# Strassen blocks in interleaved pairs, with half-bank sums, two sets of product banks and combinations on GpSimd

## The chip, the core and the metric

The kernel runs on one core of one Trainium2 chip. A core has TensorE (PE; its weight loads are shown as PEld), VectorE (DVE), ScalarE (ACT), GpSimd (POOL) and SyncE (SP, which issues DMAs). They run on their own, each takes its instructions in order, and semaphores join them. TensorE writes to PSUM alone: eight banks of 128 partitions by 512 fp32 values. ACT and DVE read PSUM, POOL doesn't. The metric is the device time of one execution in microseconds (us).

## What is computed

```python
X = np.fft.rfft(x, axis=1)                      # x: (4, 3008, 256)
Yr = Xr @ w_r - Xi @ w_i + b_r
Yi = Xr @ w_i + Xi @ w_r + b_i
Y  = shrink(Yr, 0.01) + 1j * shrink(Yi, 0.01)   # sign(v) * max(|v| - 0.01, 0)
y  = np.fft.irfft(Y, n=3008, axis=1)
h  = y.reshape(12032, 256) @ w_in               # 256 -> 2048
g  = h * sigmoid(h)                             # Silu
out = g @ w_out                                 # 2048 -> 256
```

## The kernel before

A spectral stage (DFTs as matmuls, a complex mix, the inverse DFT) feeds an MLP. The MLP takes the 12032 tokens in 24 blocks of 512 (the last, `LAST` = 23, has 256). Products are made from fp32 values split in a high and a low part (`gh`, `gl`; `win[0]`, `win[1]`), and three of the four part products are summed.

The main loop at the end of the kernel counts **ticks**: one tick is one block `i` and one `f`, a slice of 128 of the 2048 hidden features, so a block has 16 ticks. In a tick of a plain block `mlp1` makes `h` (six matmuls of 512 columns), ACT takes Silu, and in the next tick `split_g` makes `gh` (ACT) and `gl` (DVE). Then `mlp2` adds this slice to the output sums: for each 128 tokens (below: a **unit**) a 512-column matmul of `gh` with the high and the low part of `w_out` side by side (L665), and a 256-column one of `gl` (L669). So the sum of 128 tokens fills one PSUM bank, a block needs all four `acc` banks, and at the end of the block ACT copies one half and DVE adds the other (L685, L686). The banks: four `acc`, two `h`, two `d` for all else.

Spectral work for later blocks is placed in ticks by `at` and `put`: `i2` and `i2_ends` make the MLP's input of the next block (matmuls at L470; ACT and DVE split the result, and for late blocks ACT also copies it to `xf`).

The six blocks 17 to 22 (`FAST`) make `h` by Strassen's scheme: seven products of half size in place of eight. A **pair** is two `f` (q = 0 to 7), and its products live in two banks, `px` and `py`. `fast_one` (even tick) makes four products, 12 matmuls of 256 columns; then ACT copies `u` (L615) and DVE makes three sums (L616 to L618). `fast_two` (odd tick) adds three more products into the same banks, 9 matmuls, so it must wait until ACT and DVE have read them; then come a Silu (L627), two sums (L628, L629), a Silu (L630), a cast (L636), the low part (L634, called `low`), and the same for the other half (L638, L639). Both `h` banks are in use all the time. The moving combinations (`fast_moving`, once in a block: four sums on DVE, a cast on ACT, one low part on DVE) and the weight combinations (`fast_weights`, eight times before the first such block, one in each tick) are fillers too. In these blocks the sums of a tick's `f` run two ticks later, four units in every tick.

Of the kernel before, what the change touches and what calls it, by code (L numbers as in the profile page):

```python
# [116 lines left out]
def spectral_mlp_kernel(ctx: ExitStack, tc: tile.TileContext, x, w_r, w_i, b_r, b_i, w_in, w_out, c1, c2, c3, c4, c3f, c5, out):  # L117
# [24 lines left out]
    def bank(name):  # L142

        tag, bufs = "d", 2
        if state["prologue"]:
            state["d"] = (state["d"] + 1) % 4
            tag, bufs = (("d", 2), ("acc", 4), ("h", 2), ("acc", 4))[state["d"]]
        return ps.tile([128, 512], F32, tag=tag, bufs=bufs, name=name)
# [371 lines left out]
    LAST = len(BLOCKS) - 1  # L520

# [23 lines left out]
    def split_g(i, f):  # L545
# [7 lines left out]
        gf[i, f] = (gh, gl)  # L553

    HB = BLK // 2
    xf, th, tw, fast = {}, {}, {}, {}

    def fast_weights(q):

        k = slice(q * 256, (q + 1) * 256)  # L560
        f32 = tl.tile([128, 2, 256], F32, tag="td", bufs=1, name="wf")
        d = tl.tile([128, 4, 128], F32, tag="wd", bufs=2, name="wd")
# [15 lines left out]
    def fast_moving(i):  # L578
# [3 lines left out]
        l0, r0, l1, r1 = x32[:, 0, 0:HB], x32[:, 0, HB:BLK], x32[:, 1, 0:HB], x32[:, 1, HB:BLK]  # L582
        nc.vector.tensor_sub(d[:, 0, :], r0, l0)
        nc.vector.tensor_sub(d[:, 2, :], r1, r0)
        nc.vector.tensor_sub(d[:, 1, :], r1, d[:, 0, :])
        nc.vector.tensor_sub(d[:, 3, :], l1, d[:, 1, :])
        yield
        hi = tl.tile([128, 4, HB], F32R, tag="th", bufs=2, name="th")
        lo = tl.tile([128, 4, HB], F32R, tag="tl", bufs=2, name="tl")
        nc.scalar.copy(hi, d)  # L590
        yield
        nc.vector.tensor_sub(lo, d, hi)
        th[i] = (hi, lo)
# [12 lines left out]
    def fast_one(i, q):  # L606

        px, py = [ps.tile([128, 512], F32, tag="h", bufs=2, name="h") for _ in range(2)]
# [5 lines left out]
        g = tl.tile([128, 4, HB], F32, tag="gp", bufs=2, name="gp")  # L614
# [4 lines left out]
        fast[i, q] = (px, py, u, g)  # L619

    def fast_two(i, q):

        px, py, u, g = fast.pop((i, q))
# [7 lines left out]
        gs = [tuple(tl.tile([128, 2, HB], F32R, tag=f"g{k}", bufs=4, name=f"g{k}") for k in "hl") for _ in range(2)]  # L631

        def low(r):
            nc.vector.tensor_sub(gs[r][1], g[:, 2 * r:2 * r + 2, :], gs[r][0])  # L634

        nc.scalar.copy(gs[0][0], g[:, 0:2, :])  # L636
        low(0)
        nc.scalar.activation(out=g[:, 2:4, :], in_=g[:, 2:4, :], func=ACTF.Silu)  # L638
        nc.scalar.copy(gs[1][0], g[:, 2:4, :])  # L639
        later.append(lambda: low(1))  # L640
        for r in range(2):
            gf[i, 2 * q + r] = tuple(v.rearrange("p a c -> p (a c)") for v in gs[r])

    later = []
# [3 lines left out]
    def mlp2(i, f):  # L648
        n = BLOCKS[i][1]
        gh, gl = gf.pop((i, f))  # L650
        begins = f == 0 or (i, f) == (0, 8)
        ends = f == NFF - 1 or (i, f) == (0, 7)
        for t in range(n // 128):
            if begins:
                acc[i, t] = ps.tile([128, 512], F32, tag="acc", bufs=4, name="acc")
            a = acc[i, t]
            q = slice(t * 128, (t + 1) * 128)
            if i == LAST:
                for m, (v, k) in enumerate(((gh, 0), (gh, 1), (gl, 0))):
                    nc.tensor.matmul(  # L660
                        out=a[:, 0:D], lhsT=v[:, q], rhs=wout[:, f, k, :],
                        start=(f == 0 and m == 0), stop=(f == NFF - 1 and m == 2),
                    )
                continue
# [8 lines left out]
        if ends:  # L673
            for t in range(n // 128):
                a = acc.pop((i, t))
                half = x_sb[1][:, t * D:(t + 1) * D]
                if f == 7:
                    nc.scalar.copy(half, a[:, D:2 * D])
                    nc.vector.tensor_tensor(out=half, in0=a[:, 0:D], in1=half, op=ALU.add)
                    continue  # L680
                o = sb.tile([128, D], F32, tag="o", bufs=5, name="o")
                if i == LAST:
                    (nc.vector.tensor_copy if t % 2 else nc.scalar.copy)(out=o, in_=a[:, 0:D])
                else:
                    nc.scalar.copy(o, a[:, D:2 * D])  # L685
                    nc.vector.tensor_tensor(out=o, in0=a[:, 0:D], in1=o, op=ALU.add)  # L686
                if i == 0:
                    nc.vector.tensor_add(o, o, half)
                for k, b, j, p0, m in pieces(BLOCKS[i][0] + t * 128, 128):
                    v = out[b * S:(b + 1) * S].rearrange("(p j) d -> j p d", j=NJ)  # L690
                    store(v[j, p0:p0 + m, :], o[k:k + m, :])
# [50 lines left out]
    with tc.manual_schedule():  # L742
# [169 lines left out]
        for i in range(1, len(BLOCKS)):  # L912
# [6 lines left out]
            if i in FAST:  # L919
                moving = fast_moving(i)  # L920
                for k in range(3):
                    at(t + 2 + k, next, moving, None)
# [38 lines left out]
        done = 0  # L961
        for t in range(len(ticks) + 2):
            i, f = ticks[t] if t < len(ticks) else (LAST, None)
            if 0 <= t - 1 < len(ticks) and ticks[t - 1][0] not in FAST:
# [3 lines left out]
            if i in FAST:  # L968
                (fast_two if f % 2 else fast_one)(i, f // 2)
            elif t < len(ticks):  # L970
                mlp1(i, f)
            if f is None or i not in FAST or f % 2 == 0:
                while later:
                    later.pop(0)()
            for fn, args in fill.pop(t, []):
                fn(*args)
            flush(1 if t < 12 else 4)
# [33 lines left out]
```

## Time and profile before

| | |
|---|---|
| time, median of 3 runs | 1383.92 us (1381.0 to 1384.56) |
| the profiled execution | 1383.38 us; span 1381.3 us, 21395 instructions |
| PE busy | 1350.9 us, 98% of the span, granted clock 0.997 |
| DVE busy | 809.9 us, 59% |
| ACT busy | 767.9 us, 56% |
| POOL busy | 125.9 us, 9% |

The times are of one profiled execution, measured from the span's start. A matmul's duration in the trace includes the time in which its results drain, in which the next one already runs; so the distance between two starts is the pace, and the busy share of PE counts short pauses as work. A bracket at the end of a row of the timeline gives the idle time of the engine ahead of it and what ended it.

### The profile page before, as it was taken

What the parts mean: (1) busy time and instruction counts of PE and PEld (TensorE: products, weight loads), DVE (VectorE), ACT (ScalarE), POOL (GpSimd) and SP (SyncE); (2) the same over time, 40 slices, a digit from 0 to 9 for tenths busy, and PEclk for the clock granted to TensorE, in tenths of its full rate; (3) what the DMA queues carried; (4) which work ended last, traced back from release to release, by engine and by line L of the source; (5) the groups of instructions that cost most, each with busy time, mean ns of one, the idle gap of its engine ahead of it and who ended that gap; (6) DMA issues with size and microseconds to landing.
All of it is one profiled execution on the core that took longest, in us unless ns stands there. A gap on an engine that the chain in (4) does not pass through costs nothing.

```text
span 1381.3 us, 21395 instructions
## 1 busy us (share of the span) xinstructions
PE 1350.9 (98%) x8021; PEld 1175.2 (85%) x8021; DVE 809.9 (59%) x1518; ACT 767.9 (56%) x1552; POOL 125.9 (9%) x192
## 2 busy tenths in 40 slices
PE   8999999999999999999999999999999999999998
PEld 3977888888888888888888888888888888888898
DVE  3767756565665365666644455555464666666663
ACT  5446555455777455657555445554455555555554
POOL 2001002221111012221100011111000000000000
PEclk9999999999999999999999999999999999999999
DMA  8876324231543232524233212121210100010001
GB/s 266 256 228 185 111 58 117 59 89 37 128 119 99 84 88 72 143 64 104 68 88 79 67 49 80 54 77 30 59 27 7 32 28 25 3 39 16 1 16 24
DMA packets 72759, 109.81 MB, mean 79 GB/s; under 512 B 8400, under 2 KB 54224, under 8 KB 72656
## 3 DMA queue, kind: packets, MB, share of 16 engines
q1 hardware_dynamic: 58537, 79.07, 20.1%
q0 software_dynamic: 10544, 25.68, 7.2%
q10 hardware_dynamic: 3575, 3.70, 0.9%
q8 instruction: 63, 1.03, 0.3%
q14 instruction: 40, 0.33, 0.1%
HBM read 70.93 MB, written 37.49 MB: 78 GB/s over the span
## 4 chain that ended last, share of the span: by engine, by line
PE 82%; ACT 7%; DVE 6%; DMA 3%; issue 2%; DVEq 0%; SPq 0%; ACTq 0%
PE h L535 28%; PE acc L665 21%; PE acc L669 10%; PE mix L380 6%; PE h L602 5%; PE i L470 3%; PE s L355 2%; PE i L428 2%; PE mix L319 2%; ACT gh L636 1%; PE s L258 1%; DVE gp L617 1%; DVE u L616 1%; ACT gp L630 1%; DVE gp L628 1%
## 5 line engine op out<-in xcount | busy, mean ns | idle before, releaser
L665 PE MATMUL acc<-wout,gh 128*128 128x512 f32 x1472 | 540.1, 401 | 1.1 <-DVE o L686 1.1
L535 PE MATMUL h<-xt,win 128*128 128x512 f32 (+1 forms) x1728 | 436.4, 388 | 0.0
L669 PE MATMUL acc<-wout,gl 128*128 128x256 f32 x1472 | 412.4, 280 | 0.2 <-DVE gl L552 0.2
L542 ACT ACTIVATE g<-h 128x512 f32<-128x512 f32 (+1 forms) x289 | 168.7, 584 | 362.3 <-PE h L535 360.4
L535 PEld LDWEIGHTS h<-xt,win 128*128 128x128 f32 x1728 | 299.8, 188 | 61.0 <-DVE xt L487 0.4
L665 PEld LDWEIGHTS acc<-wout,gh 128*128 128x128 f32 x1472 | 277.2, 188 | 57.3 <-DVE o L686 1.7
L552 DVE TENSOR_TENSOR gl<-g,gh 128x512 fp32r<-128x512 f32 (+1 forms) x289 | 198.1, 688 | 183.5 <-ACT gh L551 180.7
L669 PEld LDWEIGHTS acc<-wout,gl 128*128 128x128 f32 x1472 | 278.0, 189 | 6.9 <-DVE gl L552 0.6
L551 ACT CAST gh<-g 128x512 fp32r<-128x512 f32 (+1 forms) x289 | 175.7, 608 | 2.8
L634 DVE TENSOR_TENSOR gl<-gp,gh 128x512 fp32r<-128x512 f32 x96 | 65.9, 687 | 39.3 <-ACT gh L636 38.8
L387 POOL TENSOR_TENSOR q<-q,bias 128x256 f32<-128x256 f32 x36 | 26.4, 734 | 570.0 <-ACT q L386 570.0
L602 PE MATMUL h<-xt,win 128*128 128x256 f32 x288 | 53.5, 294 | 16.7 <-DVE gp L617 16.6
L260 DVE TENSOR_TENSOR s1o<-s,s1o 48x512 f32<-48x512 f32 x64 | 41.0, 678 | 48.3 <-ACT s1o L259 47.3
L602 PEld LDWEIGHTS h<-xt,win 128*128 128x128 f32 x288 | 40.4, 188 | 30.2 <-issue 26.9
L627 ACT ACTIVATE gp<-h 128x256 f32<-128x256 f32 x48 | 18.4, 384 | 84.7 <-PE h L602 84.7
L487 DVE TENSOR_TENSOR xt<-i,xt 128x376 fp32r<-128x376 f32 (+2 forms) x48 | 28.1, 586 | 61.5 <-ACT xt L486 57.6
L400 DVE TENSOR_TENSOR y<-q,mix 64x256 f32<-64x256 f32 x144 | 60.3, 419 | 2.1
L470 PEld LDWEIGHTS i<-c_sb,gin 96*128 96x128 f32 x420 | 54.0, 193 | 8.0 <-issue 4.1
L365 DVE TENSOR_TENSOR xs<-s,xs 128x256 f32<-128x256 f32 x36 | 15.3, 424 | 71.9 <-ACT xs L364 71.9
L470 PE MATMUL i<-c_sb,gin 96*128 96x94 f32 x420 | 53.9, 273 | 3.1 <-DMA gin<-scr 3.1
L249 DVE TENSOR_TENSOR sx<-x_sb,sx 47x1024 fp32r<-47x1024 f32 x32 | 40.7, 1271 | 22.3 <-ACT sx L248 22.3
L188 POOL DMA_DIRECT2D x_sb<-in_x_dram x64 | 32.7, 513 | 142.6 <-ACT sx L248 125.5
(168 smaller groups left out, 1991.1 us busy)
## 6 DMA issues: line engine op xcount, KB each, us to landing
a<-scr SPq DMA_DIRECT2D x48, 256.0 KB
x_sb<-in_x_dram POOLq DMA_DIRECT2D x64, 188.0 KB, 3.5
gin<-scr SPq DMA_DIRECT2D x30, 384.0 KB
t<-in_c_dram POOLq DMA_DIRECT2D x36, 256.0 KB, 3.1
scr<-i1o SPq DMA_DIRECT2D x36, 256.0 KB
t<-in_c_dram SPq DMA_DIRECT2D x48, 128.0 KB
scr<-s1o SPq DMA_DIRECT2D x32, 192.0 KB
scr<-s1o SPq DMA_DIRECT2D x13, 384.0 KB
```

The lines of the kernel that those rows point to most:

```text
L260: nc.vector.tensor_tensor(out=o[:, c], in0=p[:2 * NR, :], in1=o[:, c], op=ALU.add)
L380: nc.tensor.matmul(out=out, lhsT=x_[:, e, c, :], rhs=m[:, e, :], start=(n == 0), stop=(n == 5))
L400: nc.vector.tensor_tensor(out=y[64 * i:64 * i + 64, r, :], in0=q[rows, i, :], in1=pv[rows, i, :], op=op,)
L470: nc.tensor.matmul(out=p[:, o:o + m], lhsT=g_t[b, j // 4][:, q:q + 128], rhs=c4_sb[:, p0:p0 + m], start=True, stop=True,)
L535: nc.tensor.matmul(out=p[:, :n], lhsT=w[:, e, f * 128:(f + 1) * 128], rhs=v[:, e, :n], start=(m == 0), stop=(m == 5),)
L542: nc.scalar.activation(out=g[:, q], in_=p[:, q], func=ACTF.Silu)
L551: nc.scalar.copy(gh[:, q], g[:, q])
L552: nc.vector.tensor_sub(gl[:, q], g[:, q], gh[:, q])
L602: nc.tensor.matmul(out=p, lhsT=w[j], rhs=m[k], start=(begins and n == 0), stop=(n == 2), skip_group_check=True,)
L634: nc.vector.tensor_sub(gs[r][1], g[:, 2 * r:2 * r + 2, :], gs[r][0])
L665: nc.tensor.matmul(out=a, lhsT=gh[:, q], rhs=wout[:, f].rearrange("p a c -> p (a c)"), start=begins, stop=False,)
L669: nc.tensor.matmul(out=a[:, D:2 * D], lhsT=gl[:, q], rhs=wout[:, f, 0, :], start=False, stop=ends,)
```

## The change

Blocks 15 to 23 (`NARROW`) keep the sums of two units in one bank: three matmuls of 256 columns write the same half bank, and the bank is emptied after its second unit by two ACT copies, with no DVE add. These blocks use two `acc` banks (`acc0`). The other two (`acc1`) are a second set for `px` and `py`: even pairs use `h`, odd pairs `acc1`. In the main loop a pair's `fast_two` is issued after the next pair's `fast_one`, with two units between; units are a list and are issued by twos. The second half of a pair's Silu, cast and low part (`parts(1)`) comes one tick later. The moving combinations go to GpSimd as eight instructions of 256 columns in eight ticks, with two ACT casts. The weight combinations are spread over more ticks (eight pairs in 11 ticks in place of 7) and use the ring of `gp` buffers, which has three in place of two.

```diff
+    NARROW = [FAST[0] - 2, FAST[0] - 1, *FAST, LAST]
...
+        def low(k):
+            nc.gpsimd.tensor_sub(lo[:, k, :], d[:, k, :], hi[:, k, :])
+
+        nc.gpsimd.tensor_sub(d[:, 0, :], r0, l0)
+        yield
+        nc.gpsimd.tensor_sub(d[:, 1, :], r1, d[:, 0, :])
+        yield
+        nc.gpsimd.tensor_sub(d[:, 2, :], r1, r0)
+        nc.scalar.copy(hi[:, 0:2, :], d[:, 0:2, :])
+        yield
+        low(0)
...
     def fast_one(i, q):
 
-        px, py = [ps.tile([128, 512], F32, tag="h", bufs=2, name="h") for _ in range(2)]
+        tag = ("h", "acc1")[q % 2]
+        px, py = [ps.tile([128, 512], F32, tag=tag, bufs=2, name="h") for _ in range(2)]
...
-    def fast_two(i, q):
-
-        px, py, u, g = fast.pop((i, q))
+        fast.append((i, q, px, py, u, g))
+
+    def fast_two():
+
+        i, q, px, py, u, g = fast.pop(0)
...
+        narrow = i in NARROW
+        k = t // 2 if narrow else t
+        if begins and not (narrow and t % 2):
+            tag = "acc0" if narrow or t % 2 == 0 else "acc1"
+            acc[i, k] = ps.tile([128, 512], F32, tag=tag, bufs=2, name="acc")
...
+        if narrow:
+            a = a[:, t % 2 * D:(t % 2 + 1) * D]
+            for m, (v, w) in enumerate(((gh, 0), (gh, 1), (gl, 0))):
+                nc.tensor.matmul(
+                    out=a, lhsT=v[:, q], rhs=wout[:, f, w, :],
+                    start=(f == 0 and m == 0 and t % 2 == 0), stop=(ends and m == 2), skip_group_check=True,
+                )
...
+        if ends and narrow and t % 2:
+            a = acc.pop((i, k))
+            for v in range(2):
                 o = sb.tile([128, D], F32, tag="o", bufs=5, name="o")
...
+                (nc.vector.tensor_copy if i == LAST and v else nc.scalar.copy)(out=o, in_=a[:, v * D:(v + 1) * D])
+                output(i, t - 1 + v, o)
...
-                at(last + 2 + q + k, next, steps, None)
-        assert last + 11 < 16 * FAST[0]
+                at(last + 2 + q * 8 // 5 + k, next, steps, None)
...
             if i in FAST:
-                (fast_two if f % 2 else fast_one)(i, f // 2)
...
+                if f % 2 == 0:
+                    fast_one(i, f // 2)
+                    if t == first_fast:
+                        run(2)
+                    else:
+                        if t > first_fast + 2:
+                            run(2)
+                        fast_two()
+                        run(2)
+                else:
+                    run(2)
+                    while later:
+                        later.pop(0)()
+                    if t > first_fast + 3:
+                        run(2)
+                fills(t)
+                continue
```

Up to the first unit of block 15 the order of every engine is the one before. Three places show what moved. The first is PE inside block 17, from the last matmul of a `fast_one` (`tl`, `sw_h`) to the first of a `fast_two` (`xt`, `win`). Before:

```order
L602 MATMUL h<-tl,sw_h_10341 128x256
L665 MATMUL acc<-wout,gh 128x512
L669 MATMUL acc<-wout,gl 128x256
L665 MATMUL acc<-wout,gh 128x512
L669 MATMUL acc<-wout,gl 128x256
L665 MATMUL acc<-wout,gh 128x512
L669 MATMUL acc<-wout,gl 128x256
L665 MATMUL acc<-wout,gh 128x512
L669 MATMUL acc<-wout,gl 128x256
L602 MATMUL h<-xt_10451,win_83 128x256 [waits DVE_49,Activation_49]
```

After:

```order
L617 MATMUL h<-tl,sw_h_10610 128x256
L682 MATMUL acc<-wout,gh 128x256 [waits Activation_49]
L682 MATMUL acc<-wout,gh 128x256
L682 MATMUL acc<-wout,gl 128x256 [waits DVE_49]
L682 MATMUL acc<-wout,gh 128x256 x2
L682 MATMUL acc<-wout,gl 128x256
L617 MATMUL h<-xt_10486,win_83 128x256
```

Two units stand there now where four stood, and the `fast_two` behind them is that of the pair before; its first matmul carries no wait.

The second place is DVE in one pair of block 17 (`u`, `gp`, `h` with their numbers, so that pairs can be told apart). Before, the sums of a `fast_one`, an old `low`, the sums of the same pair's `fast_two` and its first `low`:

```order
L616 TENSOR_TENSOR u_10988<-h_10975,u_10988 128x256 [waits PE_49,Activation_49]
L617 TENSOR_TENSOR gp_10989<-h_10974,u_10988 128x256 [waits DVE_49]
L618 TENSOR_TENSOR gp_10989<-h_10975,gp_10989 128x256 [waits DVE_49]
L634 TENSOR_TENSOR gl_10952<-gp_10918,gh_10951 128x512
L628 TENSOR_TENSOR gp_10989<-h_10974,u_10988 128x256 [waits Activation_49]
L629 TENSOR_TENSOR gp_10989<-h_10975,u_10988 128x256 [waits PE_49]
L634 TENSOR_TENSOR gl_11017<-gp_10989,gh_11016 128x512 [waits Activation_49]
```

After:

```order
L632 TENSOR_TENSOR u_11085<-h_11072,u_11085 128x256 [waits PE_49,Activation_49]
L633 TENSOR_TENSOR gp_11086<-h_11071,u_11085 128x256 [waits DVE_49]
L634 TENSOR_TENSOR gp_11086<-h_11072,gp_11086 128x256 [waits DVE_49]
L644 TENSOR_TENSOR gp_11009<-h_10994,u_11008 128x256 [waits Activation_49]
L645 TENSOR_TENSOR gp_11009<-h_10995,u_11008 128x256 [waits PE_49]
L654 TENSOR_TENSOR gl_11111<-gp_11009,gh_11110 128x512 [waits Activation_49]
L654 TENSOR_TENSOR gl_11127<-gp_11009,gh_11126 128x512 [waits DVE_49,Activation_49]
```

The two sums at L644 and L645 now belong to the pair before (11009) and stand behind the three sums of the new pair (11086).

The third place is DVE at the end of block 15, where its sums (`acc`) are emptied while weight combinations (`wf`, `wd`, `sw_l`) are made. Before:

```order
L575 TENSOR_TENSOR sw_l_10342<-wd,sw_h_10341 128x512 [waits DMAHW7_49,DMAHW0_49]
L563 TENSOR_TENSOR wf<-win_83,win_84 128x512 [waits DVE_49]
L566 TENSOR_TENSOR wd<-wf 128x128 [waits DVE_49]
L567 TENSOR_TENSOR wd<-wd,wf 128x128 [waits DVE_49]
L568 TENSOR_TENSOR wd<-wf 128x128
L569 TENSOR_TENSOR wd<-wf,wd 128x128 [waits DVE_49]
L686 TENSOR_TENSOR o<-acc,o 128x256 [waits DMAHW5_49,DMAHW6_49,DMAHW4_49,Activation_49]
```

After:

```order
L571 TENSOR_TENSOR wd<-wf,wd 128x128 [waits DVE_49]
L553 TENSOR_TENSOR gl<-g,gh 128x512 [waits PE_49,Activation_49] x2
L577 TENSOR_TENSOR sw_l_10412<-wd,sw_h_10411 128x512 [waits DMAHW7_49,DMAHW0_49,DVE_49]
L565 TENSOR_TENSOR wf<-win_83,win_84 128x2x256
L568 TENSOR_TENSOR wd<-wf 128x128 [waits DVE_49]
```

The adds of the output sums are gone from DVE, and one or two low parts (`gl`) stand between two weight combinations.

## Rows read from the trace of the kernel before

**Rows 1.** Busy time by stretch, blocks 17 to 22: start:end, us, engines, PEclk, DMA.

```profile
1056.70:1348.50 291.80, 275.11 (x1879) 248.58 (x1878) 186.70 (x405) 162.53 (x362) 0.00 (x0) 1.00 0.07 20
```

**Rows 2.** Waits, 1000 to 1381.3 us: engine line, waited for, us in total, times, longest.

```profile
PE h L602 <- DVE gp L617: 16.6, 27, 1.2
```

**Rows 3.** Timeline of PE: start, us, engine, line, operation, count, idle before.

```profile
1117.89 0.51 PE L602 MATMUL h<-xt,win 128*128 128x256 f32 x3
...
1119.32 0.40 PE L665 MATMUL acc<-wout,gh 128*128 128x512 f32 x1
...
1122.12 0.59 PE L602 MATMUL h<-xt,win 128*128 128x256 f32 x3 [1.23 <-DVE gp L617]
...
1123.26 1.03 PE L470 MATMUL i<-c_sb,gin 96*128 96x94 f32 x8
1124.07 0.47 PE L665 MATMUL acc<-wout,gh 128*128 128x512 f32 x1
...
1125.54 0.52 PE L602 MATMUL h<-xt,win 128*128 128x256 f32 x3
...
1340.17 0.40 PE L665 MATMUL acc<-wout,gh 128*128 128x512 f32 x1
...
1341.58 0.53 PE L602 MATMUL h<-xt,win 128*128 128x256 f32 x3
```

**Rows 4.** Instructions by line, 1056.7 to 1348.5 us; then line L470 there.

```profile
L665 PE MATMUL acc<-wout,gh 128*128 128x512 f32 x378 | 139.1, 402 | 0.0
...
1056.70:1348.50 291.80, 15.23 (x116) 14.43 (x116) 1.00 0.07 20
```

**Rows 5.** Timeline of ACT and of DVE around that wait.

```profile
1119.22 0.47 ACT L486 CAST xt<-i 128x376 fp32r<-128x376 f32 x1
...
1120.68 0.38 ACT L615 COPY u<-h 128x256 f32<-128x256 f32 x1
...
1123.97 0.42 ACT L630 ACTIVATE gp<-gp 128x256 f32<-128x256 f32 x1 [0.49 <-DVE gp L628]
1124.42 0.62 ACT L636 CAST gh<-gp 128x512 fp32r<-128x512 f32 x1
1124.95 0.63 ACT L638 ACTIVATE gp<-gp 128x512 f32<-128x512 f32 x1
1125.61 0.62 ACT L639 CAST gh<-gp 128x512 fp32r<-128x512 f32 x1
...
1121.09 0.42 DVE L616 TENSOR_TENSOR u<-h,u 128x256 f32<-128x256 f32 x1 [0.81 <-ACT u L615]
1121.55 0.42 DVE L617 TENSOR_TENSOR gp<-h,u 128x256 f32<-128x256 f32 x1
1122.01 0.42 DVE L618 TENSOR_TENSOR gp<-h,gp 128x256 f32<-128x256 f32 x1
1122.35 0.68 DVE L634 TENSOR_TENSOR gl<-gp,gh 128x512 fp32r<-128x512 f32 x1
1123.52 0.42 DVE L628 TENSOR_TENSOR gp<-h,u 128x256 f32<-128x256 f32 x1 [0.49 <-ACT gp L627]
...
1125.08 0.69 DVE L634 TENSOR_TENSOR gl<-gp,gh 128x512 fp32r<-128x512 f32 x1 [0.81 <-ACT gh L636]
```

**Rows 6.** Timeline of PE, end of block 15.

```profile
1013.69 1.55 PE L535 MATMUL h<-xt,win 128*128 128x512 f32 x6
1016.35 0.50 PE L665 MATMUL acc<-wout,gh 128*128 128x512 f32 x1 [1.12 <-DVE o L686]
```

**Rows 7.** One line each: duration in ns min/median/max, first and last start, forms.

```profile
L388 POOL TENSOR_TENSOR q<-q,bias x36: 741/1068/1075, 198.9 to 966.9; 128x256 f32<-128x256 f32 x36
...
L249 DVE TENSOR_TENSOR sx<-x_sb,sx x32: 1222/1222/1744, 299.3 to 741.6; 47x1024 fp32r<-47x1024 f32 x32
```

**Rows 8.** Chain that ended last, 1370 us to the end: start, us, what.

```profile
1373.56 0.72 PE acc L660 x6
...
1377.19 0.42 DVE o L683
```

More of the change, by code (lines that the diff above doesn't have):

```diff
@@ L630, in fast_two @@
         nc.scalar.activation(out=g[:, 1, :], in_=g[:, 1, :], func=ACTF.Silu)
[L631 to L640, printed above, removed]
@@ L641, in fast_two, with parts @@
-        for r in range(2):
-            gf[i, 2 * q + r] = tuple(v.rearrange("p a c -> p (a c)") for v in gs[r])
+        def parts(r):
+            h, l = [tl.tile([128, 2, HB], F32R, tag=f"g{k}", bufs=4, name=f"g{k}") for k in "hl"]
+            v = g[:, 2 * r:2 * r + 2, :]
+            if r:
+                nc.scalar.activation(out=v, in_=v, func=ACTF.Silu)
+            nc.scalar.copy(h, v)
+            nc.vector.tensor_sub(l, v, h)
+            gf[i, 2 * q + r] = tuple(a.rearrange("p a c -> p (a c)") for a in (h, l))
+            units.extend((i, 2 * q + r, t) for t in range(BLK // 128))
@@ L644, in spectral_mlp_kernel, with mlp2 @@
+        parts(0)
+        later.append(lambda: parts(1))
+    units = []
     later = []
     acc = {}
-    def mlp2(i, f):
+    def mlp2(i, f, t):
         n = BLOCKS[i][1]
-        gh, gl = gf.pop((i, f))
+        gh, gl = gf[i, f]
+        last = t == n // 128 - 1
         begins = f == 0 or (i, f) == (0, 8)
         ends = f == NFF - 1 or (i, f) == (0, 7)
[L653 to L664, printed above, removed]
+        narrow = i in NARROW
[3 more added lines that the diff above has]
+            acc[i, k] = ps.tile([128, 512], F32, tag=tag, bufs=2, name="acc")
+        a = acc[i, k]
+        q = slice(t * 128, (t + 1) * 128)
+        if narrow:
[6 more added lines that the diff above has]
+        else:
@@ L920, in spectral_mlp_kernel @@
                 moving = fast_moving(i)
[L921 to L922 removed]
+                for k in range(8):
+                    at(t + 1 + k, next, moving, None)
+                assert t + 8 < 16 * i
         for t, n in enumerate(W_GO):
@@ L957, in spectral_mlp_kernel, with fills, run @@
             for k in range(3):
-                at(last + 2 + q + k, next, steps, None)
-        assert last + 11 < 16 * FAST[0]
-        done = 0
-        for t in range(len(ticks) + 2):
+                at(last + 2 + q * 8 // 5 + k, next, steps, None)
+        assert last + 2 + 11 + 2 < 16 * FAST[0]
+        def fills(t):
+            for fn, args in fill.pop(t, []):
+                fn(*args)
+            flush(1 if t < 12 else 4)
+        def run(n):
+            for v in units[:n]:
+                mlp2(*v)
+            del units[:n]
+        first_fast, last_fast = 16 * FAST[0], 16 * (FAST[-1] + 1)
+        for t in range(len(ticks) + 1):
             i, f = ticks[t] if t < len(ticks) else (LAST, None)
-            if 0 <= t - 1 < len(ticks) and ticks[t - 1][0] not in FAST:
+            if t and ticks[t - 1][0] not in FAST:
                 split_g(*ticks[t - 1])
```

81 lines of the change are left out of this document (42 added, 39 removed).

## The prediction

> **What bounds the kernel now.** I read the busy time by stretch first, then the waits, then the timeline of PE where it waits, then ACT and DVE there. The clock is at its full 2.4 GHz level in blocks 17 to 22 (granted 1.00 [rows 1]), so pauses, not the clock, are what can be saved there. In this stretch of 291.8 us PE is busy 275.1, DVE 186.7 and ACT 162.5 [rows 1]: no engine but PE is near its limit. The view of waits puts 16.6 us on DVE's sum L617, 27 times [rows 2]: `fast_two` waits until the sums have read the banks that it adds to.
>
> A busy PE hides part of this, since a matmul's bar outlasts the start of the next. So I count work at pace, from starts. The 12 matmuls of a `fast_one` take 1119.32 - 1117.89 = 1.43 us, so a `fast_two` with 9 takes 1.07 and a pair 2.50 [rows 3]; 6 blocks of 8 pairs make 120.0. Four units take 1341.58 - 1340.17 = 1.41 us [rows 3], 0.3525 each; 378 of them [rows 4] make 133.2. The 116 matmuls at L470 [rows 4] go by eight in 0.81 us (1123.26 to 1124.07), and the four units behind them take 1.47 (to 1125.54), 0.06 more [rows 3]; with 17 such places (three per next block, two for the last) that is 11.7 + 1.0 = 12.7. Work at pace: 265.9. **PE waits 291.8 - 265.9 = 25.9 us here**, more than the view of waits says. Starts are rounded to 0.01 us, which leaves about 1.7 either way on this count.
>
> Why it waits: from the last unit at pace (1119.32 + 1.41 = 1120.73) to the `fast_two` at 1122.12 are 1.4 us [rows 3]. ACT copied `u` at 1120.68, late because it had to do the next block's input first (1119.22), and DVE's three sums follow at 1121.09, 1121.55, 1122.01 [rows 5]. Between `fast_one` and its own `fast_two` only four units cover that.
>
> **The change, part by part.**
>
> *Interleaving, second bank set.* A `fast_two` now comes after the next `fast_one`, which needs other banks. Between the sums' data and their use lie a whole pair's work, 5.4 us: the wait goes, if ACT and DVE keep up on average. What is late next? I work out two things, the cover and the ring.
>
> Cover. From the end of a `fast_two` at pace (1123.26) to the end of its first `low` (1125.08 + 0.69 = 1125.77) are 2.51 us [rows 5]. Now six units (2.16 at 0.36) and a `fast_one` (1.43) come before the first unit that reads it, and that unit's third matmul is 0.24 later: 3.83. Spare: 1.3 us. The banks are free earlier: the last sum that reads them, L629, is behind L628 (1123.52), so done about 1.0 us after the end, and the `fast_one` that takes them starts 2.16 after it. Spare: 1.1.
>
> Ring. ACT and DVE now hold each other in a ring over pairs: `u` (ACT), three sums (DVE), L628's sum of the pair before, Silu, cast, Silu, cast (ACT), next `u`. By starts in rows 5: 0.41 + 0.46 + 0.46 + 0.34 (to the next DVE operation) + 0.45 + 0.45 + 0.53 + 0.66 + 0.53 = 4.29 us. PE needs 2.50 + 8 x 0.36 = 5.38 for a pair. So in a plain pair the ring is 1.1 faster. Next-block input adds 1.46 to the ring (1119.22 to 1120.68 [rows 5]) and 0.9 to PE: 5.75 against 6.28, good. Where the output copies of a block fall in too (once per block, tick 3; four copies at the 0.38 of the `u` copy, which has their shape, 1.52), it is 7.27 against 6.28: the ring falls back 1.0, just inside the spare of 1.1 to 1.3, and the next pairs win it back. So nearly all of the 25.9 goes. I leave 2.0 us for places where the spare runs out and for the start and the end of the stretch; bounds 0 and, as a rival, 11.
>
> *Half-bank sums.* A unit is three matmuls of 256 in place of 512 + 256, the same columns and one more weight load. The last block does it already: six such matmuls, two units, in 0.72 us [rows 8], 0.36 a unit against 0.3525. Eight blocks of 64 units, 512 x 0.0075 = **3.8 us more**; at the pace of `fast_one` (1.43/12 = 0.119 a matmul) it would be 0.3575 a unit and 2.6 us, the lower bound. The weight loads stay hidden in that row. The TensorE page of the Trainium skill ("TensorE: Matmul & The Clock Gate", Back-to-back issue gap) gives N/2.4 + 2.5 ns: by it a unit would go from 325 to 327.5 ns, my estimate 1.3 us in all, and the time 1359.9; the rows show 352 and 360, and they decide.
>
> *Emptying the banks.* Four DVE adds less per block; ACT keeps four copies. At the end of block 15 PE now waits for such an add: six matmuls of 512 from 1013.69 take 1.39 at the pace of 0.23, and the next starts at 1016.35, **1.3 us late** [rows 6]. DVE was behind with the weight combinations, one in every tick. Now the add is gone and the combinations are spread: this goes, and the spreading costs nothing, since it ends before block 17 and DVE has room. With two units in a bank the first copy waits 0.36 us for the second unit; the next block's first unit is a `fast_one` and two units away, so that is hidden. At the very end it isn't: both copies read one bank now and stand one behind the other, while DVE's copy (0.42 from 1377.19 [rows 8]) had a bank of its own. **0.4 us more**, up to 0.5.
>
> *Combinations on GpSimd.* DVE loses four sums and a long low part, 2.9 us per block; ACT's cast becomes two of about 0.53 pitch. GpSimd gets eight instructions per block. The like one there takes 741 to 1075 ns [rows 7], so 5.9 to 8.6 us, over eight ticks of 2.7 (21.6). They are done before the block that needs them starts, and no other work waits on that queue by then. They may hold DVE up, below.
>
> **Sum**, against the profiled execution (1383.4; the median is 0.5 above): 1383.4 - 25.9 - 1.3 + 3.8 + 0.4 + 2.0 = 1362.4. I say **1362**.
>
> **The rivals.**
>
> *The ring binds beside the fillers.* GpSimd and DVE get in each other's way: where a GpSimd instruction ran, DVE's L249 rose from 1222 to 1744 ns, and L388 on GpSimd from 741 to 1068 [rows 7]. So a DVE operation with two inputs in SBUF (the `low`s) can be 0.5 us late. The four pairs of a block that carry the next input, the copies or combinations would lose their spare and then wait about one such hold-up: 5 blocks x 4 pairs x 0.55 = 11 us in place of 2: **1371**. For it: my ring is 1.0 over in one pair already. Against: the combinations come from tick 8 on, after that pair, where the ring is 1.1 ahead. The Trainium skill ("SBUF — State Buffer", Who interferes with whom) calls this an exclusive lock, held for a whole instruction, between GpSimd and a DVE instruction with two SBUF inputs. By that rule the later one blocks fully; the 0.52 in the row is most of one 0.74 us instruction, so the trace agrees.
>
> *The waits only move.* If PE's order still meets ACT and DVE in step (say, a `fast_one` waiting for banks as long as `fast_two` did), what goes is the 1.3, and the 3.8 and 0.4 stay: 1383.4 - 1.3 + 4.2, about **1386**, within the noise. Against: the spare of 1.1 us above.
>
> *Slower.* One mechanism: the ring becomes the pace of every pair. At my ring with fillers (4.29 + (2 x 1.46 + 1.52 + 1.84 for the block's ends, an input's half and a copy + 2 x 0.53)/8 = 5.2) it isn't; PE's mean with fillers is (120.0 + 384 x 0.36 + 12.7)/48 = 5.6. Above 5.6 each 0.1 costs 48 x 0.1 = 4.8 us. To be 0.3% slower (1387.5) takes 25.5 us, a ring of 6.2, that is 1.0 in every pair on top of the rows: two hold-ups of the size of L249's in each pair, where GpSimd has one instruction per pair on average. Time at that point: **1388**.
>
> **How the numbers follow.** Forecast, nearly all waits gone, 1358 to 1366: 0.64. Ring binds beside fillers, 1366 to 1377: 0.22. Waits move, 1379 to 1387: 0.08. Slower: 0.05. Faster than 1358: 0.01. The range takes in the bounds (1357.5: without the 2.0, with 2.6 for the units, and with 1.7 more of waits) and reaches into the second case: 1357.5 to 1372. About 0.3% is what a measurement of this kernel can tell from no change (1379.8 to 1388.1): faster 0.87, same 0.08, slower 0.05.
>
> **What would show it.** In the profile after: the stretch of blocks 17 to 22 lasts about 270 us; `fast_two` follows the units with no idle time named after DVE; four units take 1.44 us; the pause at the end of block 15 is gone; GpSimd's combinations take 0.7 to 1.1 us and no matmul waits for them. Wrong it would be if matmuls of `fast_one` or units show idle time that ends with ACT or DVE in most pairs, or if the units take more than 0.37.

## The result and the profile after

The changed kernel takes **1360.51 us** in the median of 4 runs (1358.07 to 1364.06), beside 1383.51 for the kernel before: a ratio of 0.9838, 95% interval 0.9812 to 0.9865. The profiled execution took 1361.32 us, its span is 1359.5; against the profiled execution of before that is 22.1 us less. The forecast was 1362.0 in a range of 1357.5 to 1372.0.

Two lines of the page of the kernel after: busy time by engine, and the shares of the chain that ended last.

```profile
PE 1346.2 (99%) x8533; PEld 1203.7 (89%) x8533; DVE 787.0 (58%) x1456; ACT 766.8 (56%) x1558; POOL 163.9 (12%) x240
...
PE 96%; DMA 2%; ACT 1%; DVE 0%; issue 0%; SPq 0%; ACTq 0%
```

PE has 512 matmuls more and is busy 4.7 us less: a bar lasts 0.28 us where the next start comes after 0.12, and ahead of a pause, of which there are fewer now, the rest counts as busy. The chain hardly leaves PE. The view of waits of the kernel after has no row for PE at all from 1000 us to the end, where before it had 16.6 us in 27 waits of `fast_two` [rows 2]. The stretch of blocks 17 to 22, busy time as in [rows 1]:

```profile
1056.60:1327.50 270.90, 270.90 (x2267) 270.80 (x2267) 168.72 (x356) 162.16 (x368) 31.01 (x40) 1.00 0.08 22
```

270.9 us in place of 291.8, PE busy from end to end, and the clock at 1.00 in both. The timeline of PE in block 18 of the kernel after, behind the `fast_two` of the pair that waits in [rows 3]: six units, four filler matmuls, a `fast_one`, two units, the `fast_two` of the pair before.

```profile
1119.48 0.40 PE L682 MATMUL acc<-wout,gh 128*128 128x256 f32 x2
...
1121.64 0.58 PE L470 MATMUL i2e<-c_sb,gin 96*128 96x94 f32 x4
1122.01 0.60 PE L617 MATMUL h<-xt,win 128*128 128x256 f32 x3
...
1123.52 0.40 PE L682 MATMUL acc<-wout,gh 128*128 128x256 f32 x2
...
1124.24 0.52 PE L617 MATMUL h<-xt,win 128*128 128x256 f32 x3
...
1125.32 0.40 PE L682 MATMUL acc<-wout,gh 128*128 128x256 f32 x2
```

No row has a bracket: nothing is waited for. Six units take 1121.64 - 1119.48 = 2.16, which is 0.36 each; the `fast_two` takes 1.08. ACT and DVE at the same place (compare [rows 5]):

```profile
1118.27 0.38 ACT L631 COPY u<-h 128x256 f32<-128x256 f32 x1
1119.32 0.38 ACT L643 ACTIVATE gp<-h 128x256 f32<-128x256 f32 x1 [0.68 <-PE h L617]
...
1124.08 0.39 ACT L631 COPY u<-h 128x256 f32<-128x256 f32 x1
...
1121.49 0.69 DVE L654 TENSOR_TENSOR gl<-gp,gh 128x512 fp32r<-128x512 f32 x1 [0.80 <-ACT gh L653]
```

The low part of the `fast_two` that ended at 1119.48 is done at 1121.49 + 0.69 = 1122.18, and the first matmul that reads it is the third of the unit at 1123.52, at 1123.76: 1.6 us to spare. ACT is the one that waits, 0.68 us for PE. At the end of block 15 (compare [rows 6]) the pause is gone, six matmuls of 512 columns and then the next unit 1.39 later:

```profile
1014.50 1.55 PE L536 MATMUL h<-xt,win 128*128 128x512 f32 x6
1015.89 0.40 PE L682 MATMUL acc<-wout,gh 128*128 128x256 f32 x2
```

The end of the chain that ended last (compare [rows 8]), where two copies of one bank now stand one behind the other:

```profile
1352.79 2.17 PE acc L682 x18
1354.96 0.02 issue
1354.98 0.38 ACT o L701
1355.37 0.02 issue
1355.39 0.42 DVE o L701
```

And one line each of a combination on GpSimd and of the `low`s on DVE (duration in ns min/median/max, as in [rows 7]):

```profile
L594 POOL TENSOR_TENSOR td<-xf,td x6: 735/739/1062, 1034.9 to 1261.9; 128x256 f32<-128x256 f32 x6
...
L654 DVE TENSOR_TENSOR gl<-gp,gh x96: 691/692/850, 1064.1 to 1330.4; 128x512 fp32r<-128x512 f32 x96
```

So the forecast held. Whether it held for its own reasons is what the experiments ask.

### The profile page after: what moved, and what is told of

The parts are those of the page before. It is cut to its first block, busy times and chain, and to the rows that moved or that the text cites. A ratio compares the mean times of both kernels' runs of the same rounds, so it can differ in the third digit from the quotient of the medians.

```text
span 1359.5 us, 22374 instructions
## 1 busy us (share of the span) xinstructions
PE 1346.2 (99%) x8533; PEld 1203.7 (89%) x8533; DVE 787.0 (58%) x1456; ACT 766.8 (56%) x1558; POOL 163.9 (12%) x240
## 4 chain that ended last, share of the span: by engine, by line
PE 96%; DMA 2%; ACT 1%; DVE 0%; issue 0%; SPq 0%; ACTq 0%
PE h L536 28%; PE acc L687 16%; PE acc L682 14%; PE h L617 9%; PE acc L691 8%; PE mix L380 6%; PE i L470 3%; PE s L355 2%; PE mix L319 2%; PE i L428 2%; PE s L258 1%; PE s L222 1%; PE i L425 1%; PE i2e L470 1%; PE s L298 1%; DMA t3f<-in_c3f_dram 1%
## 5 line engine op out<-in xcount | busy, mean ns | idle before, releaser
L536 PEld LDWEIGHTS h<-xt,win 128*128 128x128 f32 x1728 | 300.0, 188 | 59.5 <-DVE xt L487 0.4
L687 PE MATMUL acc<-wout,gh 128*128 128x512 f32 x960 | 352.0, 400 | 0.0
L691 PE MATMUL acc<-wout,gl 128*128 128x256 f32 x960 | 269.0, 280 | 0.1
L687 PEld LDWEIGHTS acc<-wout,gh 128*128 128x128 f32 x960 | 180.6, 188 | 37.2 <-ACT ww L752 0.3
L682 PE MATMUL acc<-wout,gh 128*128 128x256 f32 x1088 | 202.2, 283 | 0.0
L691 PEld LDWEIGHTS acc<-wout,gl 128*128 128x128 f32 x960 | 181.2, 189 | 6.2 <-DVE gl L553 0.7
L682 PEld LDWEIGHTS acc<-wout,gh 128*128 128x128 f32 x1088 | 171.0, 192 | 1.7
L682 PE MATMUL acc<-wout,gl 128*128 128x256 f32 x544 | 154.0, 283 | 0.0
L682 PEld LDWEIGHTS acc<-wout,gl 128*128 128x128 f32 x544 | 104.3, 192 | 0.1
L470 PEld LDWEIGHTS i<-c_sb,gin 96*128 96x128 f32 x420 | 54.2, 194 | 8.1 <-issue 4.1
L653 ACT CAST gh<-gp 128x512 fp32r<-128x512 f32 x96 | 59.5, 620 | 3.1
L470 PE MATMUL i<-c_sb,gin 96*128 96x94 f32 x420 | 54.4, 274 | 3.8 <-DMA gin<-scr 3.8
```

The costliest lines, as they stand in the source:

```text
L470: nc.tensor.matmul(out=p[:, o:o + m], lhsT=g_t[b, j // 4][:, q:q + 128], rhs=c4_sb[:, p0:p0 + m], start=True, stop=True,)
L536: nc.tensor.matmul(out=p[:, :n], lhsT=w[:, e, f * 128:(f + 1) * 128], rhs=v[:, e, :n], start=(m == 0), stop=(m == 5),)
L682: nc.tensor.matmul(out=a, lhsT=v[:, q], rhs=wout[:, f, w, :], start=(f == 0 and m == 0 and t % 2 == 0), stop=(ends and m == 2), skip_group ...
L687: nc.tensor.matmul(out=a, lhsT=gh[:, q], rhs=wout[:, f].rearrange("p a c -> p (a c)"), start=begins, stop=False,)
L691: nc.tensor.matmul(out=a[:, D:2 * D], lhsT=gl[:, q], rhs=wout[:, f, 0, :], start=False, stop=ends,)
```

## The experiments

The table has, for each kernel, the median, the ratio to the kernel before measured beside it on the same chip, the time from the first matmul with a combined weight (block 17) to the start of the last matmul of all, and PE's waits in blocks 17 to 22 as the view of waits names them. The third figure leaves out what earlier stages differ by.

| kernel | us | ratio (95% interval) | block 17 to the end, us | waits of PE |
|---|---|---|---|---|
| before | 1382.6 to 1385.1 | 1 | 319.7 | 16.6 us, 27 |
| after | 1360.51 | 0.9838 (0.9812 to 0.9865) | 297.6 | none |
| half banks alone | 1368.07 | 0.9891 (0.9867 to 0.9916) | 304.1 | 3.3 us, 6 |
| after, old order of pairs | 1361.34 | 0.9842 (0.9823 to 0.9862) | 298.8 | 1.1 us, 1 |
| before, ACT's order moved | 1367.56 | 0.9879 (0.9853 to 0.9906) | 303.7 | 5.0 us, 14 |
| after, ACT's order of before | 1360.35 | 0.9825 (0.9799 to 0.9851) | 297.6 | none |
| before, three small edits | 1361.06 | 0.9828 (0.9802 to 0.9853) | 298.1 | 1.8 us, 4 |
| after, combinations on DVE | 1359.86 | 0.9833 (0.9816 to 0.9851) | 297.6 | none |
| after, one more sum | 1362.18 | 0.9860 (0.9844 to 0.9877) | 299.0 | 0.4 us, 1 |
| after, three more sums | 1389.77 | 1.0051 (1.0031 to 1.0071) | 325.4 | 14.1 us, 21 |
| after, third matmul split | 1395.27 | 1.0091 (1.0062 to 1.0121) | 331.8 | none |
| before, no Strassen | 1366.96 | 0.9891 (0.9867 to 0.9916) | | none |

**Is it the interleaving? Half banks alone.** The kernel before with the new units, two to a bank, and the old order.

```diff
+    NARROW = [FAST[0] - 2, FAST[0] - 1, *FAST, LAST]
...
-        nc.scalar.copy(gs[0][0], g[:, 0:2, :])
-        low(0)
-        nc.scalar.activation(out=g[:, 2:4, :], in_=g[:, 2:4, :], func=ACTF.Silu)
-        nc.scalar.copy(gs[1][0], g[:, 2:4, :])
-        later.append(lambda: low(1))
...
+        parts(0)
+        later.append(lambda: parts(1))
```

> The kernel before with one part of the change alone: blocks 15 to 23 keep the sums of two units in one bank and empty it with two ACT copies. Pairs stand in the old order with one set of product banks; the moving combinations stay on DVE, the weight combinations in every tick. Theory (the gain is the cover that the interleaving gives fast_two): the waits of fast_two stay, the units cost 0.0075 us more each, 3.8 us; the wait at the end of block 15 may go (1.3) since no DVE add stands there: 1384 to 1388, likeliest 1386. Rival (the missing DVE adds and the free banks are the gain): 1375 or less.

Measured: 1368.07 us, 15 less than before. Of the waits of `fast_two` few are left; the row of the view of waits:

```profile
PE h L604 <- DVE gp L620: 3.3, 6, 1.1
```

The expectation failed, and it also called the edit smaller than it is: with the new units comes `parts`, and `parts(1)` takes the second half's Silu and cast into `later`, behind the next copy of `u`. Before, only the low part stood there. (The ring of `gp` has its third buffer here too.) So this run mixes edits, and either of the first two could have removed the waits.

**The old order of pairs in the kernel after.** Each `fast_two` stands behind its own `fast_one` again, four units between; the rest of the change stays, `parts(1)` in `later` too.

```diff
-                    if t == first_fast:
-                        run(2)
-                    else:
-                        if t > first_fast + 2:
-                            run(2)
-                        fast_two()
-                        run(2)
...
+                else:
+                    fast_two()
...
+                if t > first_fast:
+                    run(4)
```

> The kernel after with the order of before alone put back: a fast_two stands behind its own fast_one, with four units between. Two sets of product banks, half-bank sums and combinations on GpSimd stay. Theory: the waits of fast_two on DVE's second sum come back, nearly all of the 25.9 us but for what less DVE work takes off: 1378 to 1387, likeliest 1384. Rival (the second bank set and the relief of DVE are the gain): below 1370.

Measured: 1361.34 us, no different from the kernel after. One wait is left in blocks 17 to 22, at the first `fast_two`, which has no units ahead of it:

```profile
PE h L617 <- DVE gp L633: 1.1, 1, 1.1
```

With it the theory fell that only the interleaving gives the cover. From block 17 to the end it is worth 298.8 - 297.6 = 1.2 us here, about that one wait. What remained was ACT's order, the half banks, or the banks and GpSimd.

**ACT's order alone.** The kernel before with one thing moved.

```diff
-        nc.scalar.activation(out=g[:, 2:4, :], in_=g[:, 2:4, :], func=ACTF.Silu)
-        nc.scalar.copy(gs[1][0], g[:, 2:4, :])
-        later.append(lambda: low(1))
+        def second():
+            nc.scalar.activation(out=g[:, 2:4, :], in_=g[:, 2:4, :], func=ACTF.Silu)
+            nc.scalar.copy(gs[1][0], g[:, 2:4, :])
+            low(1)
+
+        later.append(second)
```

> The kernel before with one line moved: the second half of a pair's Silu and cast on ACT stand a tick later, behind the copy of u and with the low part that already stood there. Old order of pairs, whole-bank sums, one set of product banks, all combinations on DVE. The theory that the interleaving removes the waits has fallen with the run of the old order, where one wait was left. New theory: ACT's queue made u late (two Silus, two casts and fillers stood ahead of it), and this move lets u go as soon as its products are there: of the 25.9 us of waits all go but the 5.8 that are left in the run with half banks alone, so 1383 - 20 = 1363, with the wait at the end of block 15 still there. Rival (the half banks removed the waits: free sum banks and four DVE adds less in a block): 1380 to 1384, waits as before.

Measured: 1367.56 us, 17.5 less than the kernel before beside it (1385.07); expected were 20 less. So ACT's order is enough for most of it, without half banks; what half banks do without it was not run. The timeline of ACT between two copies of `u`, in a pair without fillers on ACT or DVE, in the kernel before:

```profile
1151.66 0.37 ACT L615 COPY u<-h 128x256 f32<-128x256 f32 x1
1154.08 0.38 ACT L627 ACTIVATE gp<-h 128x256 f32<-128x256 f32 x1 [2.05 <-PE h L602]
1154.95 0.42 ACT L630 ACTIVATE gp<-gp 128x256 f32<-128x256 f32 x1 [0.49 <-DVE gp L628]
1155.40 0.62 ACT L636 CAST gh<-gp 128x512 fp32r<-128x512 f32 x1
1155.93 0.63 ACT L638 ACTIVATE gp<-gp 128x512 f32<-128x512 f32 x1
1156.59 0.62 ACT L639 CAST gh<-gp 128x512 fp32r<-128x512 f32 x1
1157.11 0.36 ACT L615 COPY u<-h 128x256 f32<-128x256 f32 x1
```

The end of the pair of [rows 5], which has the next block's input on ACT:

```profile
1126.14 0.47 ACT L486 CAST xt<-i 128x376 fp32r<-128x376 f32 x1
1127.22 0.47 ACT L491 COPY xf<-i 128x376 f32<-128x376 f32 x1 [0.62 <-DVE xt L487]
1127.59 0.38 ACT L615 COPY u<-h 128x256 f32<-128x256 f32 x1
```

And a pair without fillers with ACT's order moved:

```profile
1146.95 0.37 ACT L615 COPY u<-h 128x256 f32<-128x256 f32 x1 [0.55 <-PE h L602]
1147.22 0.64 ACT L640 ACTIVATE gp<-gp 128x512 f32<-128x512 f32 x1
1147.89 0.62 ACT L641 CAST gh<-gp 128x512 fp32r<-128x512 f32 x1
...
1151.13 0.62 ACT L636 CAST gh<-gp 128x512 fp32r<-128x512 f32 x1
1152.30 0.37 ACT L615 COPY u<-h 128x256 f32<-128x256 f32 x1 [0.55 <-PE h L602]
```

Before, the rows close a loop through three engines: `u`, DVE's sums, `fast_two` on PE, Silu, cast, Silu, cast, next `u`, in 1157.11 - 1151.66 = 5.45 us, with no idle time ahead of `u`. PE's own work for a pair is 2.50 + 8 x 0.3525 = 5.32. So a plain pair lost 0.13 us only, some 6 us in 48 pairs by an estimate from these rows. The greater part was lost where fillers stand on the loop, since it has no room for them: with the input of the next block the pair takes 1127.59 - 1120.68 = 6.91 us, which is 5.45 and the full 1.46 of the input, where PE's work with the 0.9 of the input is 6.2. With the Silu and the cast (0.66 + 0.53 = 1.19) behind `u`, the plain pair takes 5.35, and ACT is idle 0.55 ahead of `u` and waits for PE. By starts the waits left are one at the first `fast_two` (1.3), and in each of five blocks three of 0.4, 0.6 and 0.3 us: one pair behind DVE's adds of the output sums, and twice at the moving combinations on DVE. That is 8.0; I had put in the 5.8 of the run with half banks, which has no adds. This 2.2 is most of the 2.6 by which the expectation (25.9 - 5.8 = 20.1) missed.

**The interleaving alone.** The kernel after with the second half's Silu and cast at once again.

```diff
-            nc.vector.tensor_sub(l, v, h)
-            gf[i, 2 * q + r] = tuple(a.rearrange("p a c -> p (a c)") for a in (h, l))
-            units.extend((i, 2 * q + r, t) for t in range(BLK // 128))
+
+            def low():
+                nc.vector.tensor_sub(l, v, h)
...
-        parts(0)
-        later.append(lambda: parts(1))
+        parts(0)()
+        later.append(parts(1))
```

> The kernel after with that Silu and cast back at once behind those of the first half (the low part stays a tick later), so that ACT's order within a pair is that of before and the interleaving alone has to hide it. Theory of the prediction (the ring fits and the cover is there, in whatever order ACT works): 1360.5, no or hardly any waits of a matmul. Rival (ACT's order is needed beside the interleaving too): 1366 or more, with waits of fast_two or of units.

Measured: 1360.35 us, and the view of waits names none of PE. ACT's rows there again put two Silus, two casts and a combination's cast ahead of `u`:

```profile
1136.97 0.63 ACT L652 ACTIVATE gp<-gp 128x512 f32<-128x512 f32 x1
1137.63 0.62 ACT L653 CAST gh<-gp 128x512 fp32r<-128x512 f32 x1
1138.16 0.61 ACT L604 CAST th<-td 128x512 fp32r<-128x512 f32 x1
1138.68 0.36 ACT L631 COPY u<-h 128x256 f32<-128x256 f32 x1
```

No matmul waits all the same: a `fast_two` stands behind the next `fast_one`, so the loop goes over two pairs. So the prediction's reason is enough by itself. With the rest of the change in place, so is ACT's order, and the kernel after has both. The fourth corner, the rest of the change with neither, was not run.

**Three small edits in place of the reorganization.** The kernel before with ACT's order moved, the moving combinations on GpSimd and the weight combinations spread; whole banks and the old order stay.

```diff
-                for k in range(3):
-                    at(t + 2 + k, next, moving, None)
+                for k in range(8):
+                    at(t + 1 + k, next, moving, None)
...
-                at(last + 2 + q + k, next, steps, None)
+                at(last + 2 + q * 8 // 5 + k, next, steps, None)
```

> The kernel before with ACT's order moved as in the run with that alone, the moving combinations on GpSimd and the weight combinations spread as in the kernel after; whole-bank sums, one set of product banks and the old order of pairs stay. New theory: the waits left in the run with half banks alone (4.5 us, in the pairs where the moving combinations stand on DVE) and the 1.3 at the end of block 15 go, and the 3.8 for narrow units and 0.4 at the end are not paid: 1360.5 - 4.2 is 1356 to 1358, ahead of the kernel after. Rival (without the second bank set a fast_one waits for banks, or DVE's adds bring waits back): 1360 to 1366.

Measured: 1361.06 us; the interval of the ratio covers the ratio of the kernel after. So it doesn't beat it, and my expectation was 3 to 5 too low. The units are cheaper by 384 x 0.0075 = 2.9 from block 17 on, but waits are left at 5 x 0.36 (one pair in each of five blocks) and 1.3 (the first `fast_two`), 3.1 by starts. The view of waits names 1.8 of that:

```profile
PE h L615 <- DVE gp L630: 1.8, 4, 1.1
```

The 0.36 come from the adds that whole banks need. DVE's timeline at the end of a block has all four of them ahead of the sum on which ACT's next Silu waits; then come the input and, late, `u`:

```profile
1155.98 1.41 DVE L703 TENSOR_TENSOR o<-acc,o 128x256 f32<-128x256 f32 x4
1157.31 0.41 DVE L641 TENSOR_TENSOR gp<-h,u 128x256 f32<-128x256 f32 x1
```

With half banks alone that sum stands 3.30 us behind the `u` ahead of it, here 3.98, and that run has no such wait. From block 17 to the end the kernel with three small edits takes 298.1 against 297.6. Interleaved pairs with whole-bank sums weren't tried: four `acc`, four product and two `d` banks are ten of eight. Nor were interleaved pairs with one set of product banks: a `fast_one` would need the banks that a later `fast_two` still adds to.

**GpSimd.** The kernel after with the eight instructions on DVE, in the same ticks.

```diff
-            nc.gpsimd.tensor_sub(lo[:, k, :], d[:, k, :], hi[:, k, :])
+            nc.vector.tensor_sub(lo[:, k, :], d[:, k, :], hi[:, k, :])
```

> The kernel after with the eight moving combinations of a block on DVE in place of GpSimd, in the same ticks. Theory (a block's ring has room for one DVE operation of 0.4 us in a pair, and no other wait stands there): 1359 to 1363, likeliest 1361, no matmul waits. Rival (the relief of DVE by GpSimd is needed): above 1366, with waits of units on DVE's low part.

Measured: 1359.86 us, no waits of PE. With the interleaving, moving them to GpSimd brings nothing, and costs nothing. (In the old order, in one piece on DVE, they are two of the three waits left in each block.)

**How much room has the ring?** One and three more sums on DVE in each pair, ahead of L644.

```diff
+        for n in range(3):
+            nc.vector.tensor_tensor(out=g[:, n, :], in0=px[:, HB:BLK], in1=u, op=ALU.add)
```

> The kernel after with one sum of 128x256 more on DVE in every pair, ahead of L644, in the ring of ACT and DVE (its result is overwritten by the later sums; it only costs time). Theory (cover and ring): cover takes 0.46 of the spare of 1.3; the ring goes from 5.2 to 5.67 in the mean with fillers, PE's mean is 5.64: the spare is used up by the end of the stretch or a little before, 1361 to 1364. Rival (only the latency from fast_two to the first low counts, the ring doesn't add up): no change, 1360.5.

> The kernel after with three such sums more in every pair. Theory (the ring becomes the pace): 4.29 + 1.38 in plain pairs is 5.67 against 5.38, with fillers 6.4 to 6.6 against 5.64 in the mean: 48 pairs lose 0.8 to 1.0 each, 1398 to 1406; the waits of units on the low part stand in every pair. Rival (only latency counts: 1.38 less 1.3 of spare is 0.1 in a pair): 1366 or less.

Measured: 1362.18 us with one, 1389.77 with three; 29 more than the kernel after, where 37 to 46 were expected. With three, the view of waits and DVE's timeline in one pair show

```profile
PE h L617 <- DVE gp L646: 14.1, 21, 1.2
```

```profile
1140.96 0.42 DVE L633 TENSOR_TENSOR gp<-h,u 128x256 f32<-128x256 f32 x1
1141.41 0.42 DVE L634 TENSOR_TENSOR gp<-h,gp 128x256 f32<-128x256 f32 x1
1141.76 1.08 DVE L636 TENSOR_TENSOR gp<-h,u 128x256 f32<-128x256 f32 x3
1142.75 0.41 DVE L646 TENSOR_TENSOR gp<-h,u 128x256 f32<-128x256 f32 x1
```

All 21 waits are those of a `fast_one` for its banks, not of units for a low part as expected. Three sums cost 1142.75 - 1141.76 = 0.99, or 0.33 each; 0.46, which I had taken, is the distance of sums of which one needs the other (here 1140.96 to 1141.41). Three times 0.33 is still less than the spare of 1.3 in a plain pair, so the cover is not what gave out: the ring did. From the first pair of block 18 to the first of block 22 the copies of `u` stand (1309.07 - 1106.99)/32 = 6.32 us apart, against 5.71 in the kernel after; 48 x 0.61 = 29 (from block 17 to the end 27.8, as block 22 has fewer fillers). The ring without the additions is then 6.32 - 0.99 = 5.3 in the mean with fillers; the prediction had 5.2. So in the kernel after the room is 5.7 - 5.3 = 0.4 us a pair, about one more sum, as the run with one shows.

**The end of block 15.** Block 15 in the old form (whole banks, DVE adds), once with the weight combinations spread, once in every tick.

```diff
-    NARROW = [FAST[0] - 2, FAST[0] - 1, *FAST, LAST]
+    NARROW = [FAST[0] - 1, *FAST, LAST]
...
-                at(last + 2 + q * 8 // 5 + k, next, steps, None)
+                at(last + 2 + q + k, next, steps, None)
```

> The kernel after with block 15 in the old form: a whole bank for each unit, 512-column matmuls, and DVE adds at its end. The weight combinations stay spread. Theory (the wait at the end of block 15 came from DVE being behind with the combinations): no wait there; 64 units at 0.3525 in place of 0.36 give 0.5 back, 1360. Rival (the add itself was the cause): a wait of about 1 us after the last unit of block 15, on DVE.

> As the run with block 15 in the old form, and the weight combinations in every tick too, as before the change. Theory: DVE is behind at the end of block 15 and the wait of about 1.1 to 1.3 us on its add comes back there. Rival (the wait hung on something else, say the two missing acc banks): none.

Measured (one run each): 1359.01 and 1360.18 us. Spread, no matmul waits there. In every tick the wait is back, in PE's timeline:

```profile
1012.11 1.32 PE L536 MATMUL h<-xt,win 128*128 128x512 f32 x5
1014.55 0.51 PE L682 MATMUL acc<-wout,gh 128*128 128x256 f32 x2 [1.12 <-DVE o L708]
```

In the run with half banks alone the combinations stand in every tick, the adds are gone, and there is no wait there. The kernel with three small edits has the adds with the combinations spread, and no wait there either. So the wait needs both, and either edit removes it.

**What does a narrow matmul cost?** The third matmul of each product as two of 128 columns: the same columns, 336 instructions more.

```diff
-            nc.tensor.matmul(
-                out=p, lhsT=w[j], rhs=m[k], start=(begins and n == 0), stop=(n == 2), skip_group_check=True,
-            )
+            for c in ((slice(0, 128), slice(128, 256)) if n == 2 else (slice(0, 256),)):
+                nc.tensor.matmul(
+                    out=p[:, c], lhsT=w[j], rhs=m[k][:, c], start=(begins and n == 0), stop=(n == 2),
```

> The kernel after with the third matmul of each of the 336 Strassen products (seven in a pair, 48 pairs) as two of 128 columns with the same weights: the same columns, 336 matmuls more, each with its own weight load. In the rows a 256-column matmul with its own load starts 0.120 us after the one ahead, where 256 columns at 2.4 GHz take 0.107. If the weight load (or a fixed price of an instruction) sets this pace, each matmul more costs about as much as a 94-column one in the rows, 0.11: 336 x 0.11 = 37 us, 1397. If columns set it and an instruction costs a few ns, 336 x 0.004 to 0.013 = 1 to 4 us: 1362 to 1365.

Measured: 1395.27 us, 34.8 more, and 34.2 from block 17 to the end: 0.102 us for each matmul more, at no more columns and no wait. The weight loads of a `fast_one` there, in the timeline of PEld:

```profile
1125.05 0.19 PEld L618 LDWEIGHTS h<-th,sw_l 128*128 128x128 f32 x1
1125.17 0.31 PEld L618 LDWEIGHTS h<-tl,sw_h 128*128 128x128 f32 x2
1125.40 0.19 PEld L618 LDWEIGHTS h<-th,sw_h 128*128 128x128 f32 x1
1125.51 0.19 PEld L618 LDWEIGHTS h<-th,sw_l 128*128 128x128 f32 x1
1125.63 0.31 PEld L618 LDWEIGHTS h<-tl,sw_h 128*128 128x128 f32 x2
```

From 1125.17 to 1125.63 four loads start, 0.115 apart, whether 256 or 128 columns follow. So a matmul with a load of its own costs about 0.115 to 0.12 us here, at 128 as at 256 columns. Whether the load sets this or another fixed price of a matmul can't be told apart, since every matmul here has a load. The Trainium skill ("TensorE: Matmul & The Clock Gate", LDWEIGHTS) puts a load in ns at its columns over 1.2, by which 128 would take 107, an estimate; these rows have 115.

**Was Strassen's scheme a gain at all?** The kernel before with plain products everywhere.

```diff
-FAST = range(17, 23)
+FAST = ()
```

> The kernel before with plain products in blocks 17 to 22 as in all others, and no weight combinations. Theory, by rows of before: a plain block takes about 46.7 us, a Strassen block of before 48.6, so six plain ones save 11.4, and the wait of 1.3 at the end of block 15 goes too: 1371. Strassen's scheme then was a loss before the change, and the change only makes it pay. Rival (the saved columns paid already before, waits and all): 1390 to 1397.

Measured: 1366.96 us, 16 less than before, where 12 were expected; what the other 4 are stays open. The scheme saves PE 2 x 1.39 - 2.50 = 0.28 us a pair ([rows 6] and [rows 3]), 13 in all, and before the change its waits cost more than that. In the kernel after it gains some 6 us (1366.96 - 1360.51).

## Why the prediction was right, step by step

**25.9 us of waits.** The size held. From block 17 to the end the kernel after is 319.7 - 297.6 = 22.1 us shorter; with the 2.9 that the units of these blocks cost, 25.0 of the 25.9 went, within the 1.7 either way that I gave. To count work at pace was the right reading: the view of waits named 16.6.

**Why PE waited.** Here the prediction saw a part. It put `u`'s delay to the next block's input on ACT and to four units of cover. [rows 5] already hold more: two Silus and two casts of the old pair stand ahead of `u`, and the loop of 5.45 us is longer than PE's 5.32 even in a pair without fillers, so that an input has no room on it. The change moves a Silu and a cast out of that loop, and I told of that move but gave it no price. The runs show that it alone brings 17 of the 23 us in the kernel before (16.0 of 22.1 from block 17 to the end), and that with the rest of the change in place the interleaving brings all of it without that move. The number was right since either is enough; as a story of what in the change did it, it was one of two.

**Cover.** A spare of 1.3 us was worked out; the row of a pair with fillers has 1.6, and 0.33 us more on DVE in each pair costs 299.0 - 297.6 = 1.4 us in all.

**The ring.** 4.29 us was right: where ACT and DVE catch up, five pairs into blocks 17 and 18 of the kernel after, two copies of `u` stand 4.29 and 4.32 us apart. The mean with fillers was 5.2 by the prediction, 5.3 by the run with three more sums. In the pair with the output copies `u` came 7.73 us after the one before (7.98 or 7.99 in two blocks), where PE's work is 6.28: 1.45 behind and not 1.0. It cost nothing; the `low` there was only some 0.5 late, since two of the four copies stand behind the cast that it needs.

**The left 2.0 us.** This is the term that was mis-sized: it is 0. Nothing ran out of its spare, not at the start of the stretch either, and three kernels with other work on ACT, DVE and GpSimd (after, ACT's order of before, combinations on DVE) take the same 297.6 from block 17 to the end. The rival that the waits only move, to a `fast_one`, is out with that.

**Half banks.** 0.36 us a unit, as in [rows 8], 3.8 in all. The estimate from the Trainium skill ("TensorE: Matmul & The Clock Gate", Back-to-back issue gap), 327.5 ns a unit, is not what the rows show; that section of the Trainium skill gives the gap for a matmul by itself and says that in a stream of loads and matmuls both set the spacing. The split matmuls point the same way: two of 128 columns cost 0.102 us more than one of 256.

**End of block 15 and tail.** The pause of 1.3 us is gone. The time from the last matmul's start to the end of the span grew from 1381.3 - 1376.9 = 4.4 to 1359.5 - 1354.7 = 4.8, the 0.4 of the prediction.

**GpSimd.** 0.74 us an instruction, up to 1.2 where it meets DVE; no matmul waits for it. The rival that it holds DVE up was too dear by its price: the longest `low` has 850 ns in place of 692, so 0.16 and not 0.5, once in a block, where the ring has 0.4 of room a pair. The exclusive lock of the Trainium skill ("SBUF — State Buffer", Who interferes with whom), by which the one that starts first holds the ports for its whole instruction and the other blocks, is borne out in part: in each of the five meetings with a `low` the GpSimd instruction started 0.25 us after it and took 1.2 us in place of 0.74, but the `low`, which was first, got 0.16 longer too, and no run here shows a whole instruction's length lost on DVE.

**The slower rival** named its point, a ring of 6.2 us, and a time of 1388. The run with three more sums has 6.3 and 1389.8: the mechanism and the slope were right, and the ring of the kernel after, 5.3, is 1.0 us a pair away from it.

## What to carry to other kernels

Where an engine waits once in every round, write down the whole loop that closes through all engines, and compare it with that engine's own work, with and without what else comes into it; then look in each queue on the loop for what could stand behind its next link. Moving two instructions out of the loop can bring most of what a second buffer and a new order bring. And when a change has several parts, run each remedy alone: two that are each enough look like one in the sum.

## What was not expected of the hardware

- A matmul with its own weight load cost 0.115 to 0.12 us at 128 as at 256 columns, and each split of 256 columns into 128 + 128 cost 0.102 us more. At 94 columns (L470, with 96 rows of weights) it was still 0.81/8 = 0.10 [rows 3].
- DVE's sums of 128x256 stand 0.33 us apart when they don't need each other, 0.46 when they do.
